# Decode attention with a gated FFN on one core: the FFN ends in the middle, the last value rows go straight into the transposed output, the result is stored in two column groups, and the query projection becomes a loop

## The chip, the cores and the metric

One core of a Trainium2 chip. The time is the device time of one execution in microseconds (us); a profile adds the span of the profiled execution, which is a little shorter (1281.2 us against a device time of 1282.95 for the same execution).

Names: PE is the matmul engine, DVE the vector engine, ACT the scalar engine, SP the engine that issues nearly all DMAs here. "The ring" is the on-chip buffer of four 4 MB slots through which keys and values stream. A transfer "lands" when its data is complete on the chip. The "granted clock" is the share of PE's full clock that the profile shows as allowed.

## The reference

One token, 16 query heads over 8 key/value heads, 65536 cached positions, head size 256, model width 448; beside it a gated FFN of width 1792.

```python
def _A_ref(x, k_cache, v_cache, wq, wo):          # D=448, Hq=16, Hkv=8, Sk=65536, Dh=256
    q = (x @ wq).reshape(B, Sq, Hq, Dh).transpose(0, 2, 1, 3)
    k = jnp.repeat(k_cache, 2, axis=1); v = jnp.repeat(v_cache, 2, axis=1)
    p = softmax(jnp.einsum("bhqd,bhkd->bhqk", q, k) * Dh ** -0.5)
    o = jnp.einsum("bhqk,bhkd->bhqd", p, v)
    return o.transpose(0, 2, 1, 3).reshape(B, Sq, Hq * Dh) @ wo

def _B_ref(x, w_r, w_gate, w_up, w_down):         # F=1792; with one token, "top 1" is that token
    y = (silu(x @ w_gate) * (x @ w_up)) @ w_down
    return x + y * sigmoid(x @ w_r)

xn = layernorm(x)
result = x + _A_ref(xn, ...) + _B_ref(xn, ...)
```

Keys and values are 549 MB in all with the weights, read once. There is hardly any arithmetic per byte.

## The kernel before

The kernel works through 32 turns of keys and 32 of values (four per key/value head). Phase A handles the four key turns of head 0 alone: PE transposes keys in fp32 pairs, multiplies them by the query, and frees the slot. Phase B interleaves the keys of one head with the values of the one before. Then a middle part does most of the FFN; phase C does the last four turns of values; an ending does the rest. Each engine has its own list of operations and waits (`W` is a wait for an operation of another engine or for a DMA, `O` an operation).

The order of the loads is the order of SP's list. This is the start and the end of it:

```python
item("wq", ...)                                    # 3.5 MB
for u in range(U):                                 # U = 4: keys of head 0
    for c in range(HC): slot_item("k", u, c)       # 4 MB each; waits until the slot is free
    if u == U // 2 - 1:
        item("wg", [gate -> w_area, up -> w_area], [("QT",)])    # waits until PE is done with wq
        item("wd_a", [(wd_a[:, :], wd_src(0), "wd")])            # first half of w_down
# ... cut: the turns of phase B, the values of phase C, the last slot in pieces of LAST rows
item("wd_b", [(w_area[:, 0:WDN], wd_src(1), "we0")], [("FFN1",)])  # second half of w_down, 784 KB
for i in range(rep):
    item(("wo_end", i), ...)                       # wo of the last head, 2 x 224 KB
```

The query projection is 112 static matmuls:

```python
for b in range(n):                                 # n = 112
    rr, c = divmod(b, 2 * half)
    # ... cut: offsets x0, o, lo worked out in Python
    ins = mm(ps_m[0:P, C_Q + lo:C_Q + lo + half + 1:half],
             lhsT=w_area[:, o:o + Dh].rearrange("p (x f) -> p x f", f=NH)[:, :, c % NH],
             rhs=xnT_sb[:, x0:x0 + 2], ...)
```

Values are multiplied in four column groups (`tile_position=(0, 32 * g)`), two rows of 256 per matmul, into `ps_o`. The ending copies `ps_o` out, transposes it with four small matmuls into `ps_m`, scales it, and then does the second half of the FFN's last product and the output projection:

```python
def ending():
    T = NU - 1
    dve_ob(T)                                      # PSUM -> ob_sb, 100 x 512
    pe_oT(T)                                       # 4 matmuls -> ps_m, then scale by 1/sum -> oT_sb
    pe_ffn2(1, "wd_b", w_area)                     # 7 matmuls of 448 columns
    # ... cut: waits
    O("dve", "BASE", ...)                          # base row = y * sigmoid(r) + base row
    for i in range(rep):
        O("pe", ("FIN", i), lambda it, i=i: attn_mm(ps_fin, wo_end[:, :], [i], i == 0, i == rep - 1))
    O("dve", "RESULT", ...)                        # ps_fin + base row -> bf16, 1 x 448
# SP: one store of 448 values
```

Of the kernel before, what the change touches and what calls it, by code (L numbers as in the profile page):

```python
# [11 lines left out]
NSLOT = 4  # L12
CH = 64
HC = 2
LAST = [32, 16, 8, 8]
ACT_M = (3,)
TORD = (3, 0, 1, 2)

# [1 line left out]
def bass_parallel_sum__gqa_block_cached__moe_arch_mod__decode_kernel(  # L20
# [46 lines left out]
    OROWS = 32 * (NG - 1) + 2 * rep  # L67
    SLOT = CH * Dh
    WQN, WGN, WDN, WON = RP * HqDh // 2, RP * F, FH * D, rep * NH * D
    assert WQN >= max(WGN, WDN)  # L70

    sb = []

    def S_(name, shape, dtype):
        t = nc.sbuf_tensor(name, shape, dtype)
        sb.append(t)
        return t.__enter__()
# [38 lines left out]
    xnb_f = rowsf[:, 1, :]  # L116
    base_f = rowsf[:, 2, :]
    xn_bf = S_("xn_bf", [1, D], BF16)
    res_bf = S_("res_bf", [1, D], BF16)
    stat = S_("stat", [1, 16], FP32)  # L120

    ps = []
# [9 lines left out]
    ps_q = PS_("ps_q", [P, 512], FP32)  # L132
    ps_s = PS_("ps_s", [P, 512], FP32)
    ps_sn = ps_s[:, 0:SBN * rep].rearrange("p (n i) -> p n i", i=rep)
    ps_fin = ps_s[0:1, 0:D]
    ps_o = PS_("ps_o", [P, 2 * Dh], FP32)
    ps_m = PS_("ps_m", [P, 512], FP32)
    C_XNT, C_BC, C_TOT, C_OT, C_Q, C_BIG = 0, 16, 18, 22, 28, 64
# [9 lines left out]
        sems[name] = s.__enter__()  # L148
        return name

    for n_ in ["pe", "act", "dve", "pool", "qk", "jt", "evq", "exp", "pc", "qc", "w0", "out", "wq", "wg", "wo", "wd", "we0", "we1", "we2"]:
        SEM(n_)
    for i in range(NTB):
        SEM(f"ev{i}")
# [11 lines left out]
    def W(e, *key):  # L166
        prog[e].append(("w", here[0], key, None, None))
# [10 lines left out]


    items = {}  # L180
    semtot = {}
    rounds = [0]

    def item(key, parts, need=()):
        for n in need:
            W("sp", *n)
        for ap, src, sem in parts:
            semtot[sem] = semtot.get(sem, 0) + 16
            items[key] = (sem, semtot[sem])
            prog["sp"].append(("d", here[0], ("DMA", key, len(prog["sp"])), (ap, src), sem))  # L190
# [40 lines left out]
    def wd_src(s):  # L231
        return B_w_down.rearrange("(s p t) n -> s p (t n)", s=2, p=P)[s]
# [5 lines left out]
    for u in range(U):  # L238
        for c in range(HC):
            slot_item("k", u, c)  # L240
        if u == U // 2 - 1:
            item("wg", [(w_area[:, 0:WGN // 2], flat_src(B_w_gate, F), "wg"),
                        (w_area[:, WGN // 2:WGN], flat_src(B_w_up, F), "wg")], [("QT",)])
            item("wd_a", [(wd_a[:, :], wd_src(0), "wd")])
    for t in range(NT):
        slot_item("k", t + U, 0)
        pair_item(t)
# [3 lines left out]
    for t in range(NT, NU):  # L251
# [2 lines left out]
            continue  # L254
        for c in range(HC):
            slot_item("v", t, c, last_parts(rounds[0]) if rounds[0] % NSLOT == NSLOT - 1 else None)
    item("wd_b", [(w_area[:, 0:WDN], wd_src(1), "we0")], [("FFN1",)])
    for i in range(rep):
        item(("wo_end", i), [(wo_view(wo_end[:, :])[:, i, :, :], wo_src(Hkv - 1)[:, i, :, :], "we%d" % (i + 1))])
    W("sp", "RESULT")  # L260
    prog["sp"].append(("d", here[0], ("OUT",), (out[0], res_bf[:, :]), "out"))
    items["out"] = ("out", 16)
    W("sp", "DMA", "out")

    def W_item(e, key):
        W(e, "DMA", key)
# [102 lines left out]
    def pe_setup():  # L369
        W("pe", "XE")  # L370
        W("pe", "CONST")

        def xnt(it):
            for c in range(2 * NE):
                ins = mm(ps_m[0:P, C_XNT + c:C_XNT + c + 1],
                         lhsT=xe_row[0:1, :, :, :].rearrange("o b c p -> o (b c) p")[:, c, :],
                         rhs=ident_bf[0:1, 0:1], start=True, stop=True)
            return ins

        O("pe", "XNT", xnt, n=16 * U)  # L380
        W("pe", "XNTSB")
        W_item("pe", "wq")

        def qt(it):
            half = Hq * NH // 2
            n = RP * half
            for b in range(n):
                rr, c = divmod(b, 2 * half)
                lo = c % half
                x0 = 2 * rr if c < half else 2 * NE + 2 * rr  # L390
                o = rr * HqDh + (c // NH) * Dh
                ins = mm(ps_m[0:P, C_Q + lo:C_Q + lo + half + 1:half],
                         lhsT=w_area[:, o:o + Dh].rearrange("p (x f) -> p x f", f=NH)[:, :, c % NH],
                         rhs=xnT_sb[:, x0:x0 + 2], start=(b == 0), stop=(b == n - 1), skip_group_check=True)
            return ins

        O("pe", "QT", qt)
        W("pe", "PSQ_ZERO")
        W("pe", "PSO_ZERO")
# [129 lines left out]
    def pe_V(t, c, first, last, loose=False):  # L529
        W("pe", "PC", t, c)  # L530
        if c == 0 and first:
            W("pe", "OB", t - 1)
        r, got = items[("v", t, c)]
        for k, (key, ap, o0, J) in enumerate(got):
            W_item("pe", key)

            def f(it, ap=ap, o0=o0, J=J):
                kv = ap.rearrange("p (j d) -> p j d", d=Dh)
                for j in range(0, J, 2):
                    g = (o0 + j) // 2 % NG  # L540
                    ins = mm(ps_o[32 * g:32 * g + 2 * rep, :],
                             lhsT=p_sb[:, c, o0 + j:o0 + j + 2, :].rearrange("p n i -> p (n i)"), rhs=kv[:, j:j + 2, :],
                             start=(first and c == 0 and o0 + j < 2 * NG),
                             stop=(last and c == HC - 1 and o0 + j >= CH - 2 * NG), tile_position=(0, 32 * g), skip_group_check=loose)
                return ins

            O("pe", ("PVC", t, c) if k == len(got) - 1 else ("PV", t, c, k), f)
        alias("pe", "FREE", r)
        if (t + 1) % U:
            act_pc(t + 1, c)  # L550

    def dve_ob(t):
        W("dve", "PVC", t, HC - 1)
        W("dve", "OT", min(t, NT) - 1)
        O("dve", ("OB", t), lambda it: nc.vector.tensor_copy(out=ob_sb[0:OROWS, :], in_=ps_o[0:OROWS, :]))  # L555

    def pe_oT(t):
        W("pe", "OB", t)
        W("pe", "RS", min(t, NT))

        def f(it):
            for hf in range(NH):
                c = C_OT + hf * rep
                for n2 in range(2):
                    lhsT = ob_sb[0:OROWS, n2 * Dh:(n2 + 1) * Dh].rearrange("r (p f) -> r p f", f=NH)[:, :, hf]
                    ins = mm(ps_m[0:P, c:c + rep], lhsT=lhsT, rhs=sel2_bf[0:OROWS, n2, :], start=(n2 == 0), stop=(n2 == 1))
            return ins

        O("pe", ("OT", t), f)
        W("dve", "OT", t)  # L570
        W("dve", "RS", min(t, NT))
        W("dve", "ATTN", min(t, NT) - 1)
        if t < NT:
            W_item("dve", ("wo", t // U))
        src = ps_m[0:P, C_OT:C_OT + NH * rep].rearrange("p (f i) -> p f i", f=NH)
        O("dve", ("OTSB", t), lambda it: nc.vector.tensor_tensor(out=oT_sb[:, :, :], in0=src, in1=rs[:, :, :], op=ALU.mult))
# [63 lines left out]
        O("dve", "HT", lambda it: nc.vector.tensor_copy(  # L640
            out=hT_sb[:, :, :], in_=ps_m[0:P, C_HT:C_HT + FK].rearrange("p (t s) -> p t s", s=2)))

    def pe_ffn2(s, key, area):
        W_item("pe", key)
        W("pe", "HT")

        def f(it):
            for t in range(FH):
                ins = mm(ps_y, lhsT=hT_sb[:, t, s:s + 1], rhs=area[:, t * D:(t + 1) * D],
                         start=(s == 0 and t == 0), stop=(s == 1 and t == FH - 1), skip_group_check=True)  # L650
            return ins

        O("pe", ("FFN2", s), f)
# [33 lines left out]
    def turn_B(t):  # L687
# [16 lines left out]
        pe_attn(t)  # L704
        k_JT(s1 - 1)

    def middle():
        here[0] = ("S", 1)
        pe_m1t(NU - 1)
        W("pe", "OB", NT - 1)  # L710
        O("pe", "PSO_START", lambda it: [mm(ps_o[32 * g:32 * g + 2 * rep, 0:2], lhsT=zero_bf[:, :], rhs=ident_bf[:, 0:2], start=True, stop=True,
                                            tile_position=(0, 32 * g), skip_group_check=True) for g in range(NG)][-1])
        pe_bc(NU - 1)
        pe_ffn1()
        pe_tot(NT)
        pe_ffn_hT()
        pe_ffn2(0, "wd_a", wd_a)

    def turn_C(t):
        here[0] = ("C", t - NT)  # L720
# [3 lines left out]
    def ending():  # L724
        here[0] = ("S", 2)
        T = NU - 1
        dve_ob(T)
        pe_oT(T)
        pe_ffn2(1, "wd_b", w_area)
        W("dve", "FFN2", 1)  # L730
        W("dve", "SIG")
        W("dve", "RES", NT - 1)
        O("dve", "BASE", lambda it: nc.vector.scalar_tensor_tensor(out=base_f, in0=ps_y, scalar=stat[0:1, 6:7],
                                                                  in1=base_f, op0=ALU.mult, op1=ALU.add))
        W("pe", "OTSB", T)
        W("pe", "SCOPY", NU - 1)
        for i in range(rep):
            W_item("pe", ("wo_end", i))
            O("pe", ("FIN", i), lambda it, i=i: attn_mm(ps_fin, wo_end[:, :], [i], i == 0, i == rep - 1))
        W("dve", "FIN", rep - 1)  # L740
        W("dve", "BASE")
        O("dve", "RESULT", lambda it: nc.vector.tensor_tensor(out=res_bf[:, :], in0=ps_fin, in1=base_f, op=ALU.add))  # L742

    pool_setup()
    dve_setup()
# [173 lines left out]
```

## Time and profile before

| | before |
|---|---|
| device time, first three runs | 1282.59, 1282.5, 1282.99 us |
| span of the profiled run | 1281.2 us |
| last piece of values landed | about 1272.76 us |
| store issued | 1279.63 us |
| from last values to the end | 8.4 us |

The head of the page and its DMA line. The mean rate is near all that the DMA side gives: the Trainium skill (DMA: Bandwidth & Descriptors, Where 436 GB/s comes from) states 435.2 GB/s as the ceiling of the 16 ports through which the DMA engines reach the on-chip memory, and the steady stretches here read 430 to 436.

```profile
span 1281.2 us, 22851 instructions
DMA packets 17908, 549.22 MB, mean 429 GB/s; under 512 B 1891, under 2 KB 3942, under 8 KB 4710
```

The timeline of the ending, without weight loads: start, duration, engine, line, operation, output and inputs with shapes, count, and in brackets how long the engine idled before and what ended that.

```profile
1272.80 0.60 PE L367 MATMUL ps_o<-ring,p_sb 128*4 128x512 bf16 x4 [0.66 <-DMA ring<-in_A_v_cache_dram]
1273.45 0.69 DVE L555 CAST ob_sb<-ps_o 100x512 bf16<-100x512 f32 x1 [50.85 <-PE ps_o L367]
1274.20 0.27 PE L367 MATMUL ps_m<-sel_bf,ob_sb 100*128 100x2 bf16 x4 [0.80 <-DVE ob_sb L555]
...
1274.69 2.77 PE L367 MATMUL ps_t<-w_area,hT_sb 128*1 128x448 bf16 x7 [0.22 <-DMA w_area<-in_B_w_down_dram]
1277.26 1.70 PE L367 MATMUL ps_s<-wo_end,oT_sb 128*1 128x448 bf16 x4
...
1278.99 0.61 DVE L742 TENSOR_TENSOR res_bf<-ps_s,rowsf 1x448 bf16<-1x448 f32 x1 [0.82 <-PE ps_s L367]
1279.63 0.32 SPq L791 DMA_DIRECT2D out_dram<-res_bf  x1
```

After the last values there is a string of operations, one waiting for the other. The second half of w_down lands just when PE would need it. In the chain of waits this load is the last DMA link:

```profile
1236.03 38.62 DMA w_area<-in_B_w_down_dram
1274.65 0.04 issue
1274.69 2.77 PE ps_t L367 x7
```

Some places further up in the timeline: the query projection and the first key transposes, then the key transposes at 140.60 in phase B, and those of the last slot of keys at 1194.79. The latter two start on a landing.

```profile
13.90 3.15 PE L367 MATMUL ps_m<-xnT_sb,w_area 128*128 128x2 bf16 x112 [1.63 <-ACT xnT_sb L355]
...
22.79 5.59 PE L367 MATMUL ps_t<-ident_f,ring 128*128 128x128 f32 x32 [5.74 <-DMA ring<-in_A_k_cache_dram]
...
140.60 3.68 PE L367 MATMUL ps_t<-ident_f,ring 128*128 128x128 f32 x16 [6.80 <-DMA ring<-in_A_k_cache_dram]
...
1194.79 3.68 PE L367 MATMUL ps_t<-ident_f,ring 128*128 128x128 f32 x16 [1.58 <-DMA ring<-in_A_k_cache_dram]
```

And this is the stretch where phase A ends, in the stretches view. The columns of the stretches view are: stretch, its length, busy time of PE, weight loads, DVE, ACT and POOL with counts, PE's granted clock, share of the DMA engines, GB/s. The first values of phase B are issued at 101.75.

```profile
110.00:115.00 5.00, 3.52 (x44) 2.33 (x43) 2.22 (x5) 2.74 (x4) 0.00 (x0) 1.00 1.03 446
```

### The profile page before, as it was taken

Reading aid. Unit: us, or ns where it says so; the run is one execution under the profiler, and the core shown is the slowest. Engines: PE = TensorE matmul, PEld = TensorE weight load, DVE = VectorE, ACT = ScalarE, POOL = GpSimd, SP = SyncE. Lnnn points to the kernel's source line nnn. Section 1 sums busy time; section 2 is a strip of 40 time slices with the busy share of each in tenths; the row PEclk is TensorE's granted clock in tenths of the full one; section 3 lists DMA queues with packets and bytes.
Section 4 is the critical chain, followed back from the end, with each engine's and each line's share of the span. In section 5 each row is a group of like instructions: output and inputs, shape, how many; then the busy total and the mean of one; then the engine's idle time right before and its main releaser. Section 6 shows DMA issues by size and latency. Waiting matters only on the chain.

```text
span 1281.2 us, 22851 instructions
## 1 busy us (share of the span) xinstructions
PE 971.8 (76%) x9824; PEld 668.1 (52%) x9824; DVE 584.6 (46%) x1091; ACT 459.4 (36%) x655; POOL 4.5 (0%) x35
## 2 busy tenths in 40 slices
PE   3988777788777778677797678786778876777845
PEld 3867555455454555454664445554445644445511
DVE  4756444454444454344554344553345543445300
ACT  2645333353333443224443233432334433334300
POOL 1000000000000000000000000000000000000000
PEclk9988887898888898878888889988898888889776
DMA  9999999999999999999999999999999999999997
GB/s 406 424 436 424 450 426 427 431 431 439 436 438 417 437 430 441 432 430 428 432 446 426 436 424 436 430 444 430 428 428 433 441 436 430 425 435 431 434 437 310
DMA packets 17908, 549.22 MB, mean 429 GB/s; under 512 B 1891, under 2 KB 3942, under 8 KB 4710
## 3 DMA queue, kind: packets, MB, share of 16 engines
q1 hardware_dynamic: 17890, 549.04, 99.5%
q8 instruction: 8, 0.13, 0.0%
q14 instruction: 6, 0.05, 0.0%
q10 hardware_dynamic: 4, 0.00, 0.0%
HBM read 549.03 MB, written 0.00 MB: 429 GB/s over the span
## 4 chain that ended last, share of the span: by engine, by line
DMA 69%; PE 30%; SPq 0%; ACT 0%; issue 0%; DVE 0%
DMA ring<-in_A_k_cache_dram 64%; PE ps_t L367 23%; PE ps_q L367 5%; DMA w_area<-in_B_w_down_dram 3%; DMA ring<-in_A_v_cache_dram 2%; PE ps_s L367 1%; PE ps_m L367 1%; SPq L791 0%; ACT s L445 0%; DVE res_bf L742 0%; PE ps_o L367 0%
## 5 line engine op out<-in xcount | busy, mean ns | idle before, releaser
L367 PE MATMUL ps_t<-ident_f,ring 128*128 128x128 f32 x4096 | 551.1, 290 | 118.1 <-DMA ring<-in_A_k_cache_dram 99.1
L421 DVE COPY kt_buf<-ps_t 128x1024 bf16<-128x1024 bf16 x768 | 488.3, 683 | 272.2 <-PE ps_t L367 271.8
L367 PEld LDWEIGHTS ps_t<-ident_f,ring 128*128 128x128 f32 x4096 | 478.4, 148 | 225.4 <-DMA ring<-in_A_k_cache_dram 118.5
L423 ACT ACTIVATE kt_buf<-ps_t 128x1024 bf16<-128x1024 bf16 x256 | 262.1, 1024 | 261.6 <-PE ps_t L367 261.6
L367 PE MATMUL ps_o<-ring,p_sb 128*4 128x512 bf16 x2048 | 189.5, 533 | 148.4 <-DMA ring<-in_A_v_cache_dram 148.3
L445 ACT ACTIVATE s<-ps_q 98x512 bf16<-98x512 f32 x256 | 152.9, 597 | 274.9 <-PE ps_q L367 274.9
L367 PEld LDWEIGHTS ps_o<-ring,p_sb 128*4 128x4 bf16 x2048 | 55.3, 104 | 253.9 <-issue 228.5
L367 PE MATMUL ps_q<-kt_buf,q_cur 128*2 128x512 bf16 x2048 | 164.7, 399 | 0.0
L527 DVE RECIPROCAL rs<-ps_m 128x4 f32<-128x4 f32 x29 | 5.3, 182 | 225.5 <-PE ps_m L367 225.5
L512 ACT ACTIVATE p_sb<-S_sb 128x128 bf16<-128x128 bf16 x64 | 18.9, 307 | 244.8 <-PE ps_o L367 244.5
L367 PEld LDWEIGHTS ps_s<-sel_bf,s 128*128 128x128 bf16 x1024 | 59.9, 98 | 53.8 <-ACT s L445 50.8
L367 PE MATMUL ps_s<-sel_bf,s 128*128 128x8 bf16 x1024 | 64.0, 168 | 22.6 <-ACT s L445 22.6
L555 DVE CAST ob_sb<-ps_o 100x512 bf16<-100x512 f32 x29 | 20.1, 692 | 117.6 <-PE ps_o L367 117.6
L591 DVE TENSOR_TENSOR rowsf<-ps_m,rowsf 1x448 f32<-1x448 f32 x28 | 17.1, 611 | 53.9 <-PE ps_m L367 53.9
L367 PEld LDWEIGHTS ps_m<-rowsum,ones_f 128*128 128x128 f32 x116 | 21.6, 262 | 22.3 <-issue 22.3
L367 PEld LDWEIGHTS ps_q<-kt_buf,q_cur 128*2 128x2 bf16 x2048 | 27.1, 79 | 10.1 <-issue 5.0
L367 PE MATMUL ps_m<-wo_cur,oT_sb 128*1 128x448 bf16 x112 | 25.7, 352 | 0.0
L367 PE MATMUL ps_m<-rowsum,ones_f 128*128 128x2 f32 x116 | 24.0, 312 | 0.0
L367 PEld LDWEIGHTS ps_m<-wo_cur,oT_sb 128*1 128x1 bf16 x112 | 9.3, 83 | 13.6 <-issue 1.7
L469 DVE CAST S_sb<-ps_s 128x256 bf16<-128x256 f32 x32 | 12.9, 404 | 4.3 <-PE ps_s L367 4.3
L502 ACT ACTIVATE S_sb<-S_sb,negmax 128x512 bf16<-128x512 bf16 x16 | 13.4, 864 | 3.4 <-DVE negmax L496 3.4
L471 DVE TENSOR_REDUCE m1p<-S_sb 128x2 f32<-128x256 bf16 x32 | 13.5, 421 | 1.1
(79 smaller groups left out, 137.5 us busy)
## 6 DMA issues: line engine op xcount, KB each, us to landing
ring<-in_A_k_cache_dram SPq DMA_DIRECT2D x64, 4096.0 KB, 26.4
ring<-in_A_v_cache_dram SPq DMA_DIRECT2D x2, 4096.0 KB, 32.0
ring<-in_A_v_cache_dram SPq DMA_DIRECT2D x2, 2048.0 KB, 27.5
w_area<-in_A_wq_dram SPq DMA_DIRECT2D x1, 3584.0 KB, 11.3
wo_cur<-in_A_wo_dram SPq DMA_DIRECT2D x7, 448.0 KB, 16.0
ring<-in_A_v_cache_dram SPq DMA_DIRECT2D x2, 1024.0 KB, 29.6
ring<-in_A_v_cache_dram SPq DMA_DIRECT2D x4, 512.0 KB, 30.8
w_area<-in_B_w_gate_dram SPq DMA_DIRECT2D x1, 1568.0 KB, 38.6
```

Of the source, the lines that this page charges most:

```text
L367: return pe.matmul(*a, **k)
L421: O(e, ("EV", s, m), lambda it: nc.vector.tensor_copy(out=kt[:, :], in_=tb[:, :]), f"ev{m}")
L423: O(e, ("EV", s, m), lambda it: nc.scalar.activation(out=kt[:, :], in_=tb[:, :], func=ACTF.Copy), f"ev{m}")
L445: O("act", ("EVQ", s), lambda it: nc.scalar.activation(out=s2[s % 2][0:QROWS, :], in_=ps_q[0:QROWS, :], func=ACTF.Copy), "evq")
L469: O("dve", ("SCOPY", u), lambda it: nc.vector.tensor_copy(out=S, in_=ps_sn))
L471: O("dve", ("SMAX", u), lambda it: nc.vector.tensor_reduce(out=m1p[:, :, k], in_=S.rearrange("p n i -> p i n"), axis=AX.X, op=ALU.max))
L502: O("act", ("EXP", h, i), lambda it, i=i: nc.scalar.activation(out=S_sb[:, :, i], in_=S_sb[:, :, i], func=ACTF.Exp, bias=negmax[:, i:i + 1 ...
L512: O("act", ("PC", t, c), lambda it: nc.scalar.activation(out=p_sb[:, c, :, :], in_=S_sb[:, n:n + CH, :], func=ACTF.Copy), "pc")
L527: O("dve", ("RS", t), lambda it: nc.vector.reciprocal(out=rs[:, :, :], in_=ps_m[0:P, C_TOT:C_TOT + NH * rep]))
L555: O("dve", ("OB", t), lambda it: nc.vector.tensor_copy(out=ob_sb[0:OROWS, :], in_=ps_o[0:OROWS, :]))
L591: O("dve", ("RES", t), lambda it: nc.vector.tensor_tensor(out=base_f, in0=ps_m[0:1, C_BIG:C_BIG + D], in1=base_f, op=ALU.add))
```

## The change

The intent is a shorter ending. The second half of w_down is loaded early, with the first, so that the FFN is done in the middle; the base row is put into the accumulator of the output projection there. The last two pieces of values (4 and 4 rows) are multiplied as stationary weights, which gives an already transposed output, so that the PSUM copy no longer stands behind the last values. The projection runs in two column groups of 224 and the two halves are stored by two queues. The query projection becomes a hardware loop on PE with addresses from registers.

```diff
-LAST = [32, 16, 8, 8]
+LAST = [32, 16, 8, 4, 4]
+DIRECT = 2
+NF = 2
@@ loads
-            item("wd_a", [(wd_a[:, :], wd_src(0), "wd")])
+            item("wd", [(wd_a[:, :], wd_src(0), "wd"), (wo_end[:, :], wd_src(1)[:, 0:WON], "wd"),
+                        (w_area[:, WGN:WGN + WDN - WON], wd_src(1)[:, WON:WDN], "wd")])
@@
-    item("wd_b", [(w_area[:, 0:WDN], wd_src(1), "we0")], [("FFN1",)])
@@ query projection
-            for b in range(n): ...                      # 112 static matmuls
+            mm(..., rhs=zero_bf[:, 0:NH * rep], start=True, stop=False, ...)
+            for n, c0, z0 in ((NE, 0, 0), (NE - 1, half, 2 * NE)):
+                with pe.Fori(0, n) as rr:
+                    for c in range(c0, c0 + half):
+                        lo = c % half
+                        w = w_area[:, bass.ds(rr * HqDh + (c // NH) * Dh, Dh)]
+                        mm(ps_m[0:P, C_Q + lo:C_Q + lo + half + 1:half],
+                           lhsT=w.rearrange("p (x f) -> p x f", f=NH)[:, :, c % NH],
+                           rhs=xnT_sb[:, bass.ds(rr * 2 + z0, 2)], start=False, stop=False, ...)
@@ values
+                if k > len(LAST) - 1 - DIRECT:
+                    for j in range(J):
+                        for hf in range(NH):
+                            ins = mm(ps_m[0:P, C_OT + hf * rep:C_OT + (hf + 1) * rep],
+                                     lhsT=kv[:, j, :].rearrange("p (d f) -> p d f", f=NH)[:, :, hf],
+                                     rhs=p_sb[:, c, o0 + j, :], start=False, stop=False, ...)
+                    return ins
@@ middle
-        pe_ffn2(0, "wd_a", wd_a)
+        for s in range(2):
+            pe_ffn2(s)
+        O("dve", "BASE", ...)
+        O("pe", "FIN_BASE", ...)                        # base row into the projection's accumulator
+        O("pe", "OT_ZERO", ...)
@@ ending
-        pe_ffn2(1, "wd_b", w_area)
-        ... base row, projection of 448 columns, add, one store
+        for hf in range(NH):
+            for g in range(NF):
+                ins = mm(fin(g), lhsT=oT_sb[:, hf, i:i + 1], rhs=wo[:, i, hf, g * DQ:(g + 1) * DQ], ...,
+                         tile_position=(0, 32 * g), ...)
+        O("dve", "RESULT", ... nc.vector.tensor_copy(out=res_bf[0:FROWS, :], in_=ps_s[0:FROWS, 0:DQ]))
+        # column group 0 stored by SP, column group 1 by ACT
```

(Waits and declarations are cut.)

More of the change, by code (lines that the diff above doesn't have):

```diff
@@ L69, in bass_parallel_sum__gqa_block_cached__moe_arch_mod__decode_kernel @@
     WQN, WGN, WDN, WON = RP * HqDh // 2, RP * F, FH * D, rep * NH * D
-    assert WQN >= max(WGN, WDN)
+    WD4 = WON // D
+    assert WQN >= WGN + (FH - WD4) * D and FH > WD4 and D % NG == 0
     sb = []
@@ L118, in bass_parallel_sum__gqa_block_cached__moe_arch_mod__decode_kernel @@
     xn_bf = S_("xn_bf", [1, D], BF16)
-    res_bf = S_("res_bf", [1, D], BF16)
+    res_bf = S_("res_bf", [P, D // NF], BF16)
     stat = S_("stat", [1, 16], FP32)
@@ L134, in bass_parallel_sum__gqa_block_cached__moe_arch_mod__decode_kernel @@
     ps_sn = ps_s[:, 0:SBN * rep].rearrange("p (n i) -> p n i", i=rep)
-    ps_fin = ps_s[0:1, 0:D]
+    DQ = D // NF
+    FROWS = 32 * (NF - 1) + 1
     ps_o = PS_("ps_o", [P, 2 * Dh], FP32)
@@ L149, in SEM @@
         return name
-    for n_ in ["pe", "act", "dve", "pool", "qk", "jt", "evq", "exp", "pc", "qc", "w0", "out", "wq", "wg", "wo", "wd", "we0", "we1", "we2"]:
+    for n_ in ["pe", "act", "dve", "pool", "qk", "jt", "evq", "exp", "pc", "qc", "w0", "out", "wq", "wg", "wo", "wd", "we0", "we1"]:
         SEM(n_)
@@ L180, in bass_parallel_sum__gqa_block_cached__moe_arch_mod__decode_kernel @@
     items = {}
+    late = []
     semtot = {}
@@ L256, in bass_parallel_sum__gqa_block_cached__moe_arch_mod__decode_kernel @@
             slot_item("v", t, c, last_parts(rounds[0]) if rounds[0] % NSLOT == NSLOT - 1 else None)
-    item("wd_b", [(w_area[:, 0:WDN], wd_src(1), "we0")], [("FFN1",)])
     for i in range(rep):
-        item(("wo_end", i), [(wo_view(wo_end[:, :])[:, i, :, :], wo_src(Hkv - 1)[:, i, :, :], "we%d" % (i + 1))])
-    W("sp", "RESULT")
-    prog["sp"].append(("d", here[0], ("OUT",), (out[0], res_bf[:, :]), "out"))
-    items["out"] = ("out", 16)
-    W("sp", "DMA", "out")
+        item(("wo_end", i), [(wo_view(wo_end[:, :])[:, i, :, :], wo_src(Hkv - 1)[:, i, :, :], "we%d" % i)],
+             [("FFN2", 1)] if i == 0 else ())
+    for g, e in enumerate(("sp", "act")):
+        late.append((e, g))
+    items["out"] = ("out", 16 * NF)
     def W_item(e, key):
@@ L385, in qt @@
             half = Hq * NH // 2
-            n = RP * half
-            for b in range(n):
-                rr, c = divmod(b, 2 * half)
-                lo = c % half
-                x0 = 2 * rr if c < half else 2 * NE + 2 * rr
-                o = rr * HqDh + (c // NH) * Dh
-                ins = mm(ps_m[0:P, C_Q + lo:C_Q + lo + half + 1:half],
-                         lhsT=w_area[:, o:o + Dh].rearrange("p (x f) -> p x f", f=NH)[:, :, c % NH],
-                         rhs=xnT_sb[:, x0:x0 + 2], start=(b == 0), stop=(b == n - 1), skip_group_check=True)
-            return ins
+            mm(ps_m[0:P, C_Q:C_Q + NH * rep], lhsT=ident_bf[:, :], rhs=zero_bf[:, 0:NH * rep], start=True, stop=False, skip_group_check=True)
+            for n, c0, z0 in ((NE, 0, 0), (NE - 1, half, 2 * NE)):
[5 more added lines that the diff above has]
+                           lhsT=w.rearrange("p (x f) -> p x f", f=NH)[:, :, c % NH],
+                           rhs=xnT_sb[:, bass.ds(rr * 2 + z0, 2)], start=False, stop=False, skip_group_check=True)
+            return mm(ps_m[0:P, C_Q:C_Q + NH * rep], lhsT=ident_bf[:, :], rhs=zero_bf[:, 0:NH * rep], start=False, stop=True, skip_group_check=True)
         O("pe", "QT", qt)
@@ L535, in pe_V, with f @@
             W_item("pe", key)
-            def f(it, ap=ap, o0=o0, J=J):
+            def f(it, ap=ap, o0=o0, J=J, k=k):
                 kv = ap.rearrange("p (j d) -> p j d", d=Dh)
+                if k > len(LAST) - 1 - DIRECT:
+                    for j in range(J):
+                        for hf in range(NH):
+                            ins = mm(ps_m[0:P, C_OT + hf * rep:C_OT + (hf + 1) * rep],
+                                     lhsT=kv[:, j, :].rearrange("p (d f) -> p d f", f=NH)[:, :, hf], rhs=p_sb[:, c, o0 + j, :],
+                                     start=False, stop=False, skip_group_check=True)
+                    return ins
                 for j in range(0, J, 2):
@@ L545, in f @@
                 return ins
-            O("pe", ("PVC", t, c) if k == len(got) - 1 else ("PV", t, c, k), f)
+            O("pe", ("PV", t, c, k), f)
+        alias("pe", "PVC", t, c)
         alias("pe", "FREE", r)
@@ L552, in dve_ob @@
     def dve_ob(t):
-        W("dve", "PVC", t, HC - 1)
+        W("dve", *(("PVC", t, HC - 1) if t < NU - 1 else ("PV", t, HC - 1, len(LAST) - 1 - DIRECT)))
         W("dve", "OT", min(t, NT) - 1)
@@ L565, in f @@
                     lhsT = ob_sb[0:OROWS, n2 * Dh:(n2 + 1) * Dh].rearrange("r (p f) -> r p f", f=NH)[:, :, hf]
-                    ins = mm(ps_m[0:P, c:c + rep], lhsT=lhsT, rhs=sel2_bf[0:OROWS, n2, :], start=(n2 == 0), stop=(n2 == 1))
+                    ins = mm(ps_m[0:P, c:c + rep], lhsT=lhsT, rhs=sel2_bf[0:OROWS, n2, :],
+                             start=(n2 == 0 and t < NT), stop=(n2 == 1), skip_group_check=(t >= NT))
             return ins
@@ L641, in pe_ffn_hT, with pe_ffn2 @@
             out=hT_sb[:, :, :], in_=ps_m[0:P, C_HT:C_HT + FK].rearrange("p (t s) -> p t s", s=2)))
-    def pe_ffn2(s, key, area):
-        W_item("pe", key)
+    def pe_ffn2(s):
+        W_item("pe", "wd")
         W("pe", "HT")
@@ L648, in f @@
             for t in range(FH):
-                ins = mm(ps_y, lhsT=hT_sb[:, t, s:s + 1], rhs=area[:, t * D:(t + 1) * D],
+                area, o = (wd_a, t) if s == 0 else (wo_end, t) if t < WD4 else (w_area, WGN // D + t - WD4)
+                ins = mm(ps_y, lhsT=hT_sb[:, t, s:s + 1], rhs=area[:, o * D:(o + 1) * D],
                          start=(s == 0 and t == 0), stop=(s == 1 and t == FH - 1), skip_group_check=True)
@@ L705, in turn_B, with fin @@
         k_JT(s1 - 1)
+    def fin(g):
+        return ps_s[32 * g:32 * g + 1, 0:DQ]
     def middle():
@@ L716, in middle @@
         pe_ffn_hT()
-        pe_ffn2(0, "wd_a", wd_a)
+        for s in range(2):
+            pe_ffn2(s)
+        W("dve", "FFN2", 1)
+        W("dve", "SIG")
+        W("dve", "RES", NT - 1)
+        O("dve", "BASE", lambda it: nc.vector.scalar_tensor_tensor(out=base_f, in0=ps_y, scalar=stat[0:1, 6:7],
+                                                                  in1=base_f, op0=ALU.mult, op1=ALU.add))
+        W("pe", "BASE")
+        W("pe", "SCOPY", NU - 1)
+        O("pe", "FIN_BASE", lambda it: [mm(fin(g), lhsT=ones_f[0:1, 0:1], rhs=base_f[0:1, g * DQ:(g + 1) * DQ], start=True, stop=False,
+                                           tile_position=(0, 32 * g), skip_group_check=True) for g in range(NF)][-1])
+        O("pe", "OT_ZERO", lambda it: mm(ps_m[0:P, C_OT:C_OT + NH * rep], lhsT=ident_bf[:, :], rhs=zero_bf[:, 0:NH * rep], start=True, stop=True,
+                                      skip_group_check=True))
     def turn_C(t):
@@ L728, in ending, with f @@
         pe_oT(T)
-        pe_ffn2(1, "wd_b", w_area)
-        W("dve", "FFN2", 1)
-        W("dve", "SIG")
-        W("dve", "RES", NT - 1)
-        O("dve", "BASE", lambda it: nc.vector.scalar_tensor_tensor(out=base_f, in0=ps_y, scalar=stat[0:1, 6:7],
-                                                                  in1=base_f, op0=ALU.mult, op1=ALU.add))
         W("pe", "OTSB", T)
-        W("pe", "SCOPY", NU - 1)
         for i in range(rep):
             W_item("pe", ("wo_end", i))
-            O("pe", ("FIN", i), lambda it, i=i: attn_mm(ps_fin, wo_end[:, :], [i], i == 0, i == rep - 1))
-        W("dve", "FIN", rep - 1)
-        W("dve", "BASE")
-        O("dve", "RESULT", lambda it: nc.vector.tensor_tensor(out=res_bf[:, :], in0=ps_fin, in1=base_f, op=ALU.add))
+            def f(it, i=i):
+                wo = wo_view(wo_end[:, :])
+                for hf in range(NH):
+                    for g in range(NF):
+                        ins = mm(fin(g), lhsT=oT_sb[:, hf, i:i + 1], rhs=wo[:, i, hf, g * DQ:(g + 1) * DQ], start=False,
+                                 stop=(i == rep - 1 and hf == NH - 1), tile_position=(0, 32 * g), skip_group_check=True)
+                return ins
+            O("pe", ("FIN", i), f)
+        W("dve", "FIN", rep - 1)
+        O("dve", "RESULT", lambda it: nc.vector.tensor_copy(out=res_bf[0:FROWS, :], in_=ps_s[0:FROWS, 0:DQ]))
+        for e, g in late:
+            W(e, "RESULT")
+            prog[e].append(("d", here[0], ("OUT", g), (out[0][:, g * DQ:(g + 1) * DQ], res_bf[32 * g:32 * g + 1, :]), "out"))
+        W("sp", "DMA", "out")
     pool_setup()
```

## The prediction

> **What bounds the kernel now.** DMA. The page shows 549.22 MB at a mean 429 GB/s over a 1281.2 us span; the stretches view gives DMA share 1.00 and 432 to 433 GB/s from 20 to 1180 us. The Trainium skill (DMA: Bandwidth & Descriptors, Where 436 GB/s comes from) puts the 16-engine ceiling at 435.2 GB/s; this trace agrees. PE is busy 76%, but no ring transfer lands sooner than 21.4 us after its issue (ring tile's view), so about two 4 MB slots are always queued and every engine has that slack. Only the end is latency. Timeline: last eight rows of values land about 1272.75; four PV matmuls 0.60; PSUM copy 0.69; transposing matmuls 0.27; scaling 0.16, done 1274.67; second half of w_down lands 1274.65; its seven matmuls 2.6; projection 1.70 from 1277.26; add 0.61 from 1278.99; store issued 1279.63, end 1281.2: 8.4 us after the last value, at a granted clock of 0.50.
>
> **What the change does.**
> 1. w_down's second half (784 KB) is loaded early. Equal bytes, so the queue ends at the same time (1275.2 to 1275.7), but the last values land 1.85 us later (the distance between last value and w_down in the trace): about 1274.6. Only wo (448 KB) lands behind them.
> 2. Second FFN2, the base row (0.67) and two small matmuls move to about 1223 us. They cost PE some 3 us; PE waits for values from 1230 on, with 25 us queued: free.
> 3. The last 8 rows go straight into the transposed output: 16 full-width weight loads with 2 columns each. The query projection shows 28 ns each at full clock, so 56 ns at half: 0.45 us for the last four rows plus 0.15 latency. The PSUM copy starts from the piece before and is hidden.
> 4. Projection: eight 224-column matmuls, pairs side by side. PV matmuls in four column groups take 0.43 us per four of 512 columns, so groups overlap: 4 x 0.19 + 0.3 = 1.05 instead of 1.70.
> 5. Result: a 224-column copy, about 0.37 (a 256-column cast takes 0.40), instead of 0.61.
> 6. Two stores on two queues: no gain over the 1.6 us from store issue to end, perhaps a small loss.
> 7. The query projection as a PE loop may exceed its 3.15 us; PE idles 5.8 us before the first keys and DMA slack covers more: free.
>
> **Sum.** New end: 1274.6 + 0.04 + 0.6 + 0.3 + 0.2 + 1.1 + 0.4 + 1.6 = about 1278.8 against 1281.2. The tail shrinks from 8.4 to 4.2 us; 1.85 is given back because the last value lands later. Gain 2.4 us, 0.19%, all critical. Predicted time 1280.2 us; 8-in-10 range 1278.2 to 1282.4. Faster by over 2%: 0.01; within 2%: 0.98; slower by over 2%: 0.01.
>
> **What would show it.** Chain of waits: the last DMA link becomes values (or wo), not w_down. Timeline: no w_down matmuls after the last values; last value landing about 1274.6; projection near 1.05; last DVE operation near 0.37; second-half w_down matmuls near 1225. DMA share still about 1.00 through the middle.
>
> **What would make it wrong.** A DMA rate changed by 0.2% (other order, 2 KB rows) would hide or double the gain. A far slower query loop (over 25 us) would starve the queue early. If wo landed well after the values, the projection would wait on it. Column-group switches or short stores costing half a microsecond would eat a fifth of the gain.

## The result, and the profile after

| | before | after |
|---|---|---|
| device time, four runs each | 1282.59, 1282.5, 1282.99, 1282.35 | 1280.75, 1282.19, 1281.43, 1282.7 |
| median | 1282.55 | 1281.81 |
| span of the profiled run | 1281.2 | 1279.0 |
| last values landed | about 1272.76 | 1275.01 |
| from last values to the end | 8.4 | 4.0 |

The ratio is 0.9993, with a 95% interval of 0.9976 to 1.0011: the same, at 2%. A ratio here is the mean time of one kernel's fast runs over that of the other's of the same rounds, so not quite the ratio of the medians quoted. The mean gain is 0.84 us (1282.61 against 1281.77), but the four times of after spread over 2 us where those of before spread over 0.6. The profiled run of after is the fastest of the four. All outputs are right.

The page's head and DMA line:

```profile
span 1279.0 us, 23059 instructions
DMA packets 18342, 549.22 MB, mean 429 GB/s; under 512 B 1942, under 2 KB 3992, under 8 KB 5144
```

The same bytes; more packets, since the last pieces have shorter rows. The timeline of the ending:

```profile
1274.44 0.37 PE L372 MATMUL ps_m<-p_sb,ring 128*128 128x2 bf16 x8
1274.48 0.69 DVE L568 CAST ob_sb<-ps_o 100x512 bf16<-100x512 f32 x1 [47.20 <-PE ps_o L372]
1275.05 0.37 PE L372 MATMUL ps_m<-p_sb,ring 128*128 128x2 bf16 x8 [0.24 <-DMA ring<-in_A_v_cache_dram]
1275.44 0.26 PE L372 MATMUL ps_m<-sel_bf,ob_sb 100*128 100x2 bf16 x4
...
1275.95 0.91 PE L372 MATMUL ps_s<-wo_end,oT_sb 128*1 128x224 bf16 x8 [0.26 <-DVE oT_sb L590]
1276.91 0.38 DVE L773 CAST res_bf<-ps_s 33x224 bf16<-33x224 f32 x1 [1.01 <-PE ps_s L372]
1277.32 0.32 SPq L826 DMA_DIRECT2D out_dram<-res_bf  x1
1277.32 0.23 ACTq L826 DMA_DIRECT2D out_dram<-res_bf  x1
```

The copy now runs beside the two direct pieces. The seven w_down matmuls are gone from here, the projection takes 0.91 us instead of 1.70, the last DVE operation 0.38 instead of 0.61. The chain of waits ends on values now:

```profile
1238.30 36.71 DMA ring<-in_A_v_cache_dram
1275.01 0.04 issue
1275.05 0.37 PE ps_m L372 x8
```

Further up in the timeline, the query projection has become seven groups like the first two below (one per loop iteration), and the key transposes start ten microseconds later:

```profile
14.01 2.10 PE L372 MATMUL ps_m<-xnT_sb,w_area 128*128 x16 [0.18 <-issue]
...
16.59 2.10 PE L372 MATMUL ps_m<-xnT_sb,w_area 128*128 x16 [0.48 <-issue]
...
32.88 2.37 PE L372 MATMUL ps_t<-ident_f,ring 128*128 128x128 f32 x10 [1.29 <-issue]
...
143.43 2.82 PE L372 MATMUL ps_t<-ident_f,ring 128*128 128x128 f32 x12 [4.26 <-DMA ring<-in_A_k_cache_dram]
...
1197.05 1.97 PE L372 MATMUL ps_t<-ident_f,ring 128*128 128x128 f32 x16 [1.58 <-DMA ring<-in_A_k_cache_dram]
```

From the first zeroing matmul at 13.64 to the query being out at 31.59 it is 17.95 us, where the static form took 3.15. The landings at 140.60 and 1194.79 have moved to 143.43 and 1197.05; some 2 us of that is the w_down that now goes ahead of them. The first values are issued 5.9 us later than before (107.65 against 101.75), and the stretches view shows PE without a pause and a dip of the DMA rate where phase A ends:

```profile
110.00:115.00 5.00, 5.00 (x58) 4.02 (x57) 3.71 (x7) 3.19 (x4) 0.00 (x0) 1.00 0.84 341
```

So the trace of the fastest run shows nearly what was predicted, an end at 1279.0 against 1278.8. The question is why the mean gain was only 0.84 us. Two explanations were open: chance from run to run (theory A), or a cost of the change elsewhere in the stream, with the loop or the earlier w_down as suspects (theory B).

### The profile page after: what moved, and what is told of

The parts are those of the page before. It is cut to its first block, busy times and chain, and to the rows that moved or that the text cites. A ratio compares the mean times of both kernels' runs of the same rounds, so it can differ in the third digit from the quotient of the medians.

```text
span 1279.0 us, 23059 instructions
## 1 busy us (share of the span) xinstructions
PE 984.8 (77%) x9859; PEld 674.4 (53%) x9859; DVE 584.2 (46%) x1091; ACT 459.6 (36%) x655; POOL 4.6 (0%) x35
## 4 chain that ended last, share of the span: by engine, by line
DMA 65%; PE 33%; issue 1%; DVE 0%; SPq 0%; ACT 0%; ACTq 0%
DMA ring<-in_A_k_cache_dram 59%; PE ps_t L372 24%; PE ps_q L372 6%; DMA ring<-in_A_v_cache_dram 5%; PE ps_m L372 2%; PE ps_s L372 1%; DMA wr_row<-in_B_w_r_dram 0%; SPq L826 0%; ACT s L450 0%; DVE rowsf L340 0%; DVE xe_row L335 0%; DVE stat L312 0%; DVE rowsf L342 0%; DVE rowsf L319 0%; ACTq L826 0%
## 5 line engine op out<-in xcount | busy, mean ns | idle before, releaser
L372 PE MATMUL ps_o<-ring,p_sb 128*4 128x512 bf16 x2040 | 193.1, 545 | 144.5 <-DMA ring<-in_A_v_cache_dram 144.4
L372 PE MATMUL ps_m<-xnT_sb,w_area 128*128 x112 | 14.7, 184 | 2.8 <-issue 2.8
L372 PEld LDWEIGHTS ps_m<-xnT_sb,w_area 128*128 x112 | 11.7, 104 | 5.8 <-issue 3.3
```

The source lines that it names most:

```text
L372: return pe.matmul(*a, **k)
```

## The experiments

Each call ran its kernels and the kernel before on one chip; the three calls landed on three different chips. Before itself had means of 1282.92, 1282.81 and 1282.88 us there, with a spread of 0.7, 1.0 and 0.7 us over nine runs. No difference between variants below reaches 2%, and the 95% intervals of the ratios are about 0.14% wide to each side, so what is read from means below a microsecond is always read together with the trace or with the list of runs.

| run | mean minus before, us | all its runs, us |
|---|---|---|
| after_again | -2.10 | 1280.88, 1280.51, 1280.56, 1281.43, 1280.7 |
| after_unrolled | -2.20 | 1281.01, 1280.46, 1280.55, 1280.6, 1280.96 |
| before_loop | +1.27 | 1283.93, 1284.18, 1284.79, 1284.21, 1283.83 |
| ffn_move_only | -0.66 | 1282.2, 1282.28, 1282.52, 1282.13, 1282.14 |
| query_twice | +15.2 | 1297.7, 1298.1, 1297.62, 1298.42 |
| no_direct | -0.77 | 1281.39, 1282.49, 1282.11, 1282.17, 1282.03 |
| one_group | -0.25 | 1282.46, 1281.96, 1281.98, 1283.59, 1282.79 |
| one_queue | -2.01 | 1281.05, 1280.6, 1280.7, 1280.72, 1280.93 |
| after_third | -1.07 | 1283.53, 1280.94, 1282.77, 1281.29, 1280.52 |
| unrolled_again | -2.04 | 1280.69, 1280.9, 1281.14, 1280.92, 1280.55 |
| warm | -2.12 | 1280.78, 1280.33, 1280.72, 1280.94, 1281.02 |
| finer_warm | -1.76 | 1282.21, 1280.32, 1281.13, 1280.69, 1281.23 |

In each list the first time is that of the profiled execution.

### after_again: the changed kernel once more

No edit.

> The changed kernel itself, again. Theory A (the whole effect is the tail, 2.2 us shorter in the traces, and the four timed runs, spread over 2 us, merely hide it): mean 1.5 to 2.5 us below before in the same rounds, last values landing within 0.5 us of 1275.0 in the trace. Theory B (the 18 us query loop, or the earlier w_down, makes the DMA stream end later by about 1 us on average): mean only 0.3 to 1.2 us below before and a spread over 1.5 us where before spreads 0.6. Theory C (a real gain of nil): within 0.3 us.

Measured: a median of 1280.7 us, 2.10 us below before in the mean; ratio 0.9983, interval 0.9970 to 0.9997. The trace has its last values at 1275.13. On this chip theory A's number comes out, and theory C is excluded.

### after_unrolled: the change without the query loop

```diff
-            for n, c0, z0 in ((NE, 0, 0), (NE - 1, half, 2 * NE)):
-                with pe.Fori(0, n) as rr: ...
+            for b in range(n): ...        # the 112 static matmuls of before
```

> The changed kernel with the query projection unrolled as before (112 matmuls, 3.15 us instead of 17.95). Theory A: same as the changed kernel within 0.4 us; first key transpose back at 22.8 us, nothing gained by it. Theory B with the loop as the culprit: 0.7 to 1.5 us faster than the changed kernel, and its runs within 0.6 us of each other.

Measured: 2.20 us below before, ratio 0.9982, and within 0.1 us of the changed kernel beside it. The query takes 3.15 us again and the transposes start at 22.68. So on this chip the loop cost nothing that could be measured in the mean; the five unrolled runs lie within 0.55 us, the five with the loop beside them within 0.92.

### before_loop: the query loop alone, in the kernel before

```diff
-            for b in range(n): ...
+            ... the loop of the change
```

> The kernel before with only its query projection turned into the loop. Theory A: equal to before within 0.4 us, though the first key transposes start at about 32.8 instead of 22.8 us. Theory B with the loop as the culprit: 0.7 to 1.5 us slower than before and a spread of over 1.5 us.

Measured: 1.27 us slower than before; its fastest run (1283.83) is above the slowest of nine runs of before (1283.28). Here the loop does cost. Its stretches view shows where:

```profile
110.00:115.00 5.00, 5.00 (x58) 4.03 (x57) 3.77 (x6) 3.12 (x5) 0.00 (x0) 1.00 0.74 315
```

And its timeline shows the two landings:

```profile
142.15 1.97 PE L367 MATMUL ps_t<-ident_f,ring 128*128 128x128 f32 x16 [1.83 <-DMA ring<-in_A_k_cache_dram]
...
1196.08 1.97 PE L367 MATMUL ps_t<-ident_f,ring 128*128 128x128 f32 x16 [3.31 <-DMA ring<-in_A_k_cache_dram]
```

PE is busy without a pause there (5.00 of 5.00) and frees the slots late; SP issues the first values at 108.41 instead of 101.75, and the DMA engines fall to a share of 0.74 in these five microseconds. (The view counts a packet whole in the stretch in which it starts, so short stretches mislead: it shows 0.18 from 110 to 112. With each packet spread over its recorded duration, the share is 0.38 from 108 to 109, 0.53 from 109 to 110, and 0.99 from 110 on. The queue ran dry just before the values were issued.) How PE came to be late is in the chains of waits, at the fifth slot of keys. Before:

```profile
33.38 37.63 DMA ring<-in_A_k_cache_dram
71.01 0.04 issue
71.06 5.35 PE ps_t L367 x32
```

With the loop:

```profile
77.15 0.56 issue
77.71 5.35 PE ps_t L367 x32
```

The kernel before has a pause of 4.14 us here, in which PE waits for this slot. With the loop PE starts the first slot 10.1 us later (32.93 instead of 22.79), and most of the pause vanishes, which takes up 3.5 us of the delay; the other 6.65 us stay, and by them the first values are issued later.

The key landing at 140.60 before comes at 142.15, 1.55 us later, and 1.29 of it is still there at the last keys, 1196.08 against 1194.79. The stream never makes it up, because it has no idle time to make it up in. (The expected spread of over 1.5 us did not come: these five runs lie within 0.96 us.)

This split theory B: the loop is harmful or harmless depending on what else is queued. The change also loads 784 KB more ahead of this point, which at 429 GB/s is 1.87 us of transfer. That pays for a dry spell of this size. This is theory B': the loop brings the queue to the edge of running dry at the end of phase A, and the early w_down happens to cover it, not always fully. Up to this point the changed kernel differs from before_loop in the early w_down alone (the other changes lie at the end), so the two traces can be compared.

### ffn_move_only: the move of the FFN alone

```diff
-LAST = [32, 16, 8, 4, 4]
-DIRECT = 2
-NF = 2
+LAST = [32, 16, 8, 8]
+DIRECT = 0
+NF = 1
+... query projection static, one store by SP
```

(The diff is against the changed kernel.)

> Before plus only the move: w_down's second half loaded early, second FFN2 and base row in the middle (base row put into PSUM ahead of the projection); no direct rows, one column group, one store, query unrolled. Theory A: tail after the last values 0.60 + 0.75 + 0.3 + 0.2 + 1.7 + 0.6 + 1.6 = about 5.9 us instead of 8.4, last values 1.85 later, so about 0.7 us faster than before. If the earlier w_down harms the DMA stream: same or slower than before, with the last values landing later than 1275.3.

Measured: 0.66 us faster than before (0.77 by medians). In the trace the last values land at 1274.60, 1.84 us later than before, and the end comes at 1280.4, 5.8 us after them. Both are as expected: the early w_down does not harm the stream, and the move is worth only the difference of 2.6 us of matmuls and 1.84 us of later landing.

### query_twice: the loop run twice in the changed kernel

```diff
         def qt(it):
+            qt_once(it)
+            return qt_once(it)
```

(The first pass is overwritten by the second, so the result stays right.)

> The changed kernel with the query loop run twice (same result, the first pass is overwritten): query done about 18 us later, first key transposes at about 51 us. Theory A (all in the tail, start-up has slack to spare): unchanged within 0.4 us, as the queue still holds ten microseconds. Theory B' (the loop is harmless only while the queue does not run dry where the keys-only phase ends, near 110 us; the loop alone cost 1.2 us in the kernel before, with a stretch at DMA share 0.18 there, and the early w_down pays 1.9 us of it back): PE is behind by another 8 to 18 us there, so a gap of 5 to 18 us with DMA share near 0 between 50 and 130 us, and the time rises by 5 to 18 us over the changed kernel.

Measured: 1297.9 us, 15.2 us above before. Theory A's slack to spare is not there: 18 us more before the first transposes cost about 17 us in the end. In its stretches view PE is busy throughout, and the DMA engines starve:

```profile
110.00:120.00 10.00, 10.00 (x114) 8.05 (x112) 7.54 (x12) 6.24 (x9) 0.00 (x0) 1.00 0.65 279
120.00:130.00 10.00, 10.00 (x114) 8.05 (x113) 8.20 (x14) 6.23 (x9) 0.00 (x0) 1.00 0.31 111
```

So the slack at the start is about as large as the one loop uses up, and nearly all of what goes beyond it is lost.

### no_direct: without the direct rows

```diff
-DIRECT = 2
+DIRECT = 0
```

> The changed kernel with no direct rows (the pieces stay 32, 16, 8, 4, 4, all in the four-group accumulator). The PSUM copy (0.69 us plus handshakes 0.06) comes back behind the last values and the last piece takes 0.6 instead of 0.38: 0.9 to 1.0 us slower than the changed kernel; projection and copy unchanged at 0.93 and 0.38. If the direct path were no gain: within 0.3 us.

Measured: 0.77 us below before, and 1.24 above one_queue. Both carry the query loop, whose scatter is in these means, so the trace is the better witness. In its chain of waits:

```profile
1274.69 0.61 PE ps_o L372 x2
1275.30 0.02 issue
1275.33 0.70 DVE ob_sb L568
```

The copy is behind the last values again. From the start of the last piece's matmuls to the store (1274.69 to 1277.96) it is 3.27 us; with direct rows it is 2.27 (1275.05 to 1277.32 in the changed kernel). The direct path is worth 1.0 us, as expected.

### one_group: one column group and one store

```diff
-NF = 2
+NF = 1
-    for g, e in enumerate(("sp", "act")):
+    for g, e in enumerate(("sp", "act")[:NF]):
```

> The changed kernel with one column group of 448 and one store. Projection back from 0.93 to about 1.65 us, result copy from 0.38 to 0.61: 0.9 to 1.0 us slower than the changed kernel. If the second store or the 448-byte rows had cost something, less: 0.5 us.

Measured: 0.25 us below before, so 1.76 above one_queue in the mean, more than expected. Its trace holds two separate things. One is the ending, in the timeline:

```profile
1276.82 1.65 PE L372 MATMUL ps_s<-wo_end,oT_sb 128*1 128x448 bf16 x4 [0.26 <-DVE oT_sb L590]
1278.51 0.61 DVE L773 CAST res_bf<-ps_s 1x448 bf16<-1x448 f32 x1 [1.75 <-PE ps_s L372]
```

From the last piece's matmuls to the store it is 3.26 us (1275.89 to 1279.15), 1.0 more than in the changed kernel, as expected. The other 0.7 to 0.8 us is that the last values land at 1275.84 in this trace, while they land between 1274.94 and 1275.13 in the good ones. Of this, 0.46 us is there at the last keys (1197.39 against 1196.93 in unrolled_again), long before the column groups are used, so that part belongs to the scatter of the stream; where the rest comes from was not tested. That column groups work side by side, as the Trainium skill states (TensorEngine Tiling (Array Packing), Key Properties: different tiles can execute in parallel), agrees: eight matmuls of 224 columns took 0.91 us, four of 448 took 1.65.

### one_queue: both stores by SP

```diff
-    for g, e in enumerate(("sp", "act")):
+    for g, e in enumerate(("sp", "sp")):
```

> The changed kernel with both stores issued by SP, one after the other. The second issue starts 0.37 us later (an issue takes 0.32): 0.3 to 0.4 us slower than the changed kernel. If the queues serialise elsewhere anyway: equal within 0.1 us.

Measured: 2.01 us below before. From the first store's issue to the end of the span it is 1.9 us, against 1.7 with two queues; in the mean of runs no loss can be told apart. The Trainium skill (DMA: Bandwidth & Descriptors, Issuing engines are not separate DMA queues) says that issuing from several engines only saves the issuing time; a second issue of 0.3 us is what there was to save, and the trace shows 0.2 of it. The second queue is nearly worthless here.

### after_third and unrolled_again: the scatter

No edit in the first; the second is after_unrolled again. They ran on the same chip in the same rounds.

> The changed kernel a third time, for the spread of its first four runs (1280.75 to 1282.7) against 0.6 us for before. If the query loop leaves the queue on the edge of running dry near 110 us, some runs here are 1 to 2 us longer than the unrolled version beside it; if those first runs were only a matter of that chip or hour, its mean is within 0.3 us of the unrolled version and 2.0 to 2.4 below before.

> The changed kernel with the query projection unrolled, again, as the neighbour of the other three: 2.0 to 2.4 us below before, runs within 0.6 us of each other.

Measured: the changed kernel is 1.07 us below before, its runs spread over 3.0 us; the unrolled one is 2.04 below, its runs spread over 0.6. And here the profiled execution of the changed kernel was the bad one, 1283.53 us, which shows when the time is lost. The unrolled kernel's timeline has the two landings at:

```profile
142.52 3.67 PE L372 MATMUL ps_t<-ident_f,ring 128*128 128x128 f32 x16 [6.60 <-DMA ring<-in_A_k_cache_dram]
...
1196.93 2.81 PE L372 MATMUL ps_t<-ident_f,ring 128*128 128x128 f32 x16 [3.59 <-DMA ring<-in_A_k_cache_dram]
```

The changed kernel's bad execution has them at:

```profile
144.56 1.76 PE L372 MATMUL ps_t<-ident_f,ring 128*128 128x128 f32 x7 [3.94 <-DMA ring<-in_A_k_cache_dram]
...
1199.20 0.98 PE L372 MATMUL ps_t<-ident_f,ring 128*128 128x128 f32 x7 [1.59 <-DMA ring<-in_A_k_cache_dram]
```

The same landing is 2.04 us later at 144 us, and still 2.27 us later at the last keys. Most of the whole lateness is there within the first 145 us. (Some 0.9 us more was lost between the last keys and the last values, 1278.1 against 1274.9; its cause is not settled.) In the good executions of the changed kernel the same landing is only 0.6 to 0.9 us late at 143 us and the delay has shrunk to about 0.1 at 1197.

### warm and finer_warm: keeping PE's clock up in the ending

Both start from after_unrolled.

```diff
+WARM = (30, 16, 12)
@@ values, phase C
+            if t > NT and (t - NT) % 2 and c == HC - 1 and k < len(WARM):
+                O("pe", ("WARM", t, k), lambda it, k=k: [mm(ps_q[:, 0:P], lhsT=ident_bf[:, :], rhs=ident_bf[:, :],
+                                                         start=True, stop=True) for _ in range(WARM[k])][-1])
@@ finer_warm, besides
-LAST = [32, 16, 8, 4, 4]
-DIRECT = 2
+LAST = [32, 16, 8, 4, 2, 2]
+DIRECT = 3
```

> Unrolled, plus 30, 16 and 12 dummy matmuls of 128 columns into an unused PSUM bank in PE's waits before the pieces of 32, 16 and 8 rows. If the half clock (granted 0.50) sets the length of the last PE work, the projection falls from 0.91 to about 0.6 us, the last direct piece from 0.37 to about 0.28 and the transposing four from 0.26 to 0.22: 0.3 to 0.5 us faster than unrolled. If fixed latencies set it, under 0.15 us.

> As the warm one, with the last piece of 4 rows split into 2 and 2 (three direct pieces). The work after the last landing falls by four more weight loads, 0.1 to 0.2 us; but the second half of wo lands about 1 us after the last values, so the projection should start to wait for it and the gain over the warm one stay under 0.15 us.

Measured: 2.12 and 1.76 us below before; neither is faster than unrolled_again beside them (2.04) by more than 0.1. The timeline of warm:

```profile
1268.59 2.83 PE L373 MATMUL ps_q<-ident_bf 128*128 128x128 bf16 x30
...
1274.94 0.55 PE L373 MATMUL ps_m<-p_sb,ring 128*128 128x2 bf16 x16
1275.81 0.25 PE L373 MATMUL ps_m<-sel_bf,ob_sb 100*128 100x2 bf16 x4 [0.31 <-DVE ob_sb L572]
1276.32 0.55 PE L373 MATMUL ps_s<-wo_end,oT_sb 128*1 128x224 bf16 x8 [0.26 <-DVE oT_sb L594]
```

The clock does set the projection's length: 0.55 us instead of 0.91. This agrees with the Trainium skill (TensorE: Matmul & The Clock Gate, What's actually happening), which gives 1.2 GHz for an idle and 2.4 GHz for a busy array: the granted clock from 1275.90 to 1276.90 is 1.00 here and 0.50 in unrolled_again. But the thirty dummies met a slow PE (granted clock 0.50 before them) and took 2.83 us, more than the wait that they were to fill (2.29 us in unrolled_again); PE fell behind, the copy of the accumulator ended later, and it was the copy again that released the transposing matmuls (1275.81, after DVE, instead of 1275.37). What was gained in one place was given back in the other. The expectation failed on the number of dummies; the idea of a warm PE stays open, with an estimated 0.4 us in it at most (0.91 less 0.55 for the projection). finer_warm shows nothing beyond that; its profiled run, 1282.21 us, reached the last keys on time (1196.70) and lost its time later. The traces show where: after the middle the next values were issued at 1233.16 instead of 1231.84 in warm, the DMA rate from 1231 to 1237 us was 349 GB/s instead of 497, and the last landing in its chain of waits is 1.47 us later (1266.41 against 1264.94), about what its end is later (1280.4 against 1279.0).

## Why the prediction was right or wrong

The measured time, 1281.81 us, lies in the range given, and "within 2%" was right. The centre, 1280.2, was 1.6 us too low for the first four runs, and 0.5 too low for the five of after_again.

- **What bounds the kernel: right.** The DMA stream, and then a string of latencies. What shortens the string shows in the time microsecond for microsecond.
- **Step 1, early w_down: right, and a little small.** The last values land later by 1.84 us in ffn_move_only and by about 2.2 in the unrolled kernels (1274.94 against 1272.76), where 1.85 was said. What was loaded late is loaded early, so this part is always given back.
- **Step 2, the FFN in the middle: not as free as was said.** PE resumed the values at 1228.07 instead of 1223.5, 4.5 us later rather than 3, since the second seven matmuls and the base row ran one after the other there. The queue was not full then: the next values were issued at 1231.79 instead of 1227.79. In the fastest trace the DMA rate from 1231 to 1237 us held (503 GB/s, 475 before), but where that issue came at 1233.2 to 1233.4 it fell to 358 (after_again), 341 (one_queue) and 349 (finer_warm). The first two lost nothing by it (78.1 and 78.0 us from the last keys to the last values, 78.0 in the kernel before); finer_warm ends 1.4 us later than warm. So the margin here is small too; no run isolates it.
- **Step 3, direct rows: right.** The last piece took 0.37 us (0.6 was summed), and the path is worth 1.0 us by no_direct.
- **Steps 4 and 5, column groups and copy: right.** 0.91 and 0.38 us, where 1.05 and 0.37 were said; 1.0 us together by one_group.
- **Step 6, two stores: right.** About 1.7 us from issue to the end, against 1.6 before.
- **The sum: right for an undisturbed run.** An end at 1278.8 was predicted; the undisturbed traces end at 1278.9 (both unrolled ones) and 1279.0.
- **Step 7, "PE idles 5.8 us before the first keys and DMA slack covers more: free": wrong.** This is the failed step. The loop took 17.95 us. Alone it costs 1.27 us (before_loop). Run twice it costs 17 us (query_twice). In the changed kernel it is covered by the 784 KB that the same change queues earlier, and only just: the fourteen runs of the changed kernel range from 1280.51 to 1283.53, the ten unrolled runs with the same ending from 1280.46 to 1281.14. That is where much of the expected gain went: means 0.84, 2.10 and 1.07 us with the loop, 2.20 and 2.04 without. It is not the only source of scatter (finer_warm, with the static projection, spreads over 1.9 us), and three of the four runs of the result were not profiled. That the early w_down, meant for the ending, pays for the loop was luck: the prediction did not count on it.
- **Why step 7 failed.** The prediction took the shortest time from issue to landing, 21.4 us, for slack "on every engine", and warned of starvation only beyond 25 us. That time tells how long a transfer waits in the queue, not how late its issue may be. In phase A, PE consumes keys no faster than they arrive (10.1 us per 4 MB slot, from the issue at 101.75 to that at 111.82 in the trace of before, where 4 MB at 430 GB/s take an estimated 9.8), so a late start of PE stays a late freeing of slots and a late issue to the end of phase A, except for what the one pause of 4.14 us takes up: 10.1 us at the start, 6.7 at the first values. The shortest time to landing in before_loop is 16.2 us, and the queue still ran dry beside it, with a share of 0.38 from 108 to 109 us.

What stays open: why the same loop costs 2 us in some executions and nothing in others. From 110 to 115 us the stretches view does not sort the good from the bad (the fastest and the slowest profiled run of the changed kernel both read 341 GB/s), but that stretch is too short for it. With each packet's bytes spread over its recorded duration, from 104 to 122 us, the six profiled executions with the static projection move 433 GB/s, as if nothing had happened. Those with the loop run once fall short of that by an estimated 0.0 us (no_direct), 0.1 (one_queue), 0.3 (after_again), 0.7 (after), 0.9 (one_group), 1.3 (after_third) and 1.9 us (before_loop). The shortfall tends to grow with the time at which the first values are issued, 107.51 in no_direct and 108.52 in after_third, where the static ones issue them by 104.63. So it looks as if a microsecond of PE's timing decides, which no run isolates; what moves it, and why 0.9 us more was lost at the end of after_third, was not tested.

The version with the change and the static query projection (after_unrolled) is as fast as the changed kernel's best runs and does not scatter. It is the one to keep: 2.1 us, 0.17%, below before.

## What to carry to other kernels

In a kernel that streams at the DMA limit, moving work and bytes away from the end gains only what is not itself pushed back: loading 784 KB earlier made the last values land 1.84 us later, and most of the gain came from shortening the string of operations behind them. Check a "free" slowdown at the start against the first phase in which the engine is busy without a pause, not against how deep the queue looks on average; what ran dry once in this saturated stream stayed lost nearly whole (1.29 of 1.55 us at the last keys). When a change bundles a gain with a small unrelated rewrite, run the rewrite alone: it may be masked by the rest, and show only as scatter.

## What the Trainium skill lacked or had wrong

- Cost of a matmul whose operand addresses come from registers, in a PE loop (TensorE: Matmul & The Clock Gate has no figure): sixteen took 2.10 us, 131 ns each, against 28 ns each for the static ones (3.15 us for 112), plus 0.39 to 0.48 us of idle between two iterations.
- DMA: Bandwidth & Descriptors, Where 436 GB/s comes from, says without a condition that the HBM side (about 358 GB/s) binds transfers from HBM to the on-chip memory, though the page says elsewhere that a core alone gets more; with one core running, 430 to 436 GB/s were held here for over a millisecond, near the fabric figure of the same section.
- No page was found that says how queue depth turns into slack: transfers needed at least 16.2 us from issue to landing in before_loop, and the DMA engines still fell to a share of 0.38 from 108 to 109 us beside them.
